# A chain of unread instructions behind the last store of a four-layer attention kernel

## The chip, the cores and the metric

The kernel runs on one core of a Trainium2 chip. The metric is the device time of one execution in microseconds (us); the time before is the median of two runs. TensorE is called PE in the profile, its weight loads PEld, VectorE DVE, ScalarE ACT, GpSimd POOL and the queue of SyncE SP.

## The reference

Two blocks alternate over one sequence of 2048 tokens of width 512, with 32 heads of 16: a block A of linear attention and a block B of sliding-window attention over the last 256 positions, each behind a layer norm and with a residual.

```python
def _A_ref(x, wqkv, wo):            # qkv split into q, k, v per head
    phi = lambda t: jnp.where(t > 0, t + 1, jnp.exp(t)) + 1e-6
    pq, pk = phi(q), phi(k)
    kv = jnp.einsum("bhsd,bhse->bhde", pk, v)
    z = jnp.einsum("bhsd->bhd", pk)
    num = jnp.einsum("bhqd,bhde->bhqe", pq, kv)
    den = jnp.einsum("bhqd,bhd->bhq", pq, z)[..., None] + 1e-6
    return merge_heads(num / den) @ wo
def _B_ref(x, wqkv, wo):            # W = 256
    scores = jnp.einsum("bhqd,bhkd->bhqk", q, k) * (Dh ** -0.5)
    mask = (idx[:, None] - idx[None, :] >= 0) & (idx[:, None] - idx[None, :] < W)
    p = _softmax(jnp.where(mask[None, None], scores, -1e9), axis=-1)
    return merge_heads(jnp.einsum("bhqk,bhkd->bhqd", p, v)) @ wo
x = A_x
x = x + _A_ref(_layernorm(x), A_wqkv, A_wo)
x = x + _B_ref(_layernorm(x), B_wqkv, B_wo)
x = x + _A_ref(_layernorm(x), A_wqkv, A_wo)
return x + _B_ref(_layernorm(x), B_wqkv, B_wo)
```

## The kernel before

Everything stays in the on-chip memory: the residual (`xres`), queries (`XQ`), keys (`kB`), values (`vB`), the exponentials of the scores (`pb`, later also `vp`) and all weights (`wA`, `wBp`, `wBv`, `wBo`). The 2048 tokens are 16 tiles of 128. A graph of operations is built by `layer_a_keys`, `barrier` and `middle`; a stored table gives the order of all operations, the engine of those that could go to two, and the bank of the accumulators (`ps`, eight banks of 128 x 512 f32). `synchronise` works out which semaphore counts each operation must wait for, and `play` in `run` issues the operations of one engine in that order: waits first, then the instruction, which raises its engine's semaphore by one (`sems`) or, for a transfer, a semaphore of its own (`dsem` for SP's, `osem` for the 15 output tiles that POOL issues).

The operations whose durations are used later are these. `tok` (L369) makes a 128x512 product from four matmuls with 512 columns each; `feat` (L383) makes it from 16 matmuls with 128 columns. `b_scores` (L599) and `b_far` (L632) multiply blocks of 32 rows, four of them at once, one in each quarter of the array's rows (`tile_position=(32 * gq, 0)`). `den` (L506) uses 32 columns of the array for each of four tiles (`tile_position=(0, 32 * tg)`). `b_values` (L674) uses the whole array with only 34 moving columns. On ACT, L609 and L641 are the exponentials of the scores, L392 the one of `phi`, L358 copies. On DVE, L615 and L650 are masks, L393 and L394 the two steps of `phi`, L537 the residual. On POOL, L649 is the mask by position, L301, L289 and L316 set up constants, L332 and L333 are parts of the layer norm.

The output leaves in 17 transfers: 15 tiles by POOL (L783) as they become ready, and the last tile in two halves by SP (L727). When SP has played its list, it waits for the last use of every one of its 48 transfer semaphores and for all of `osem`; the other engines have no such wait. The program ends when all five engines have ended their blocks. Before its first operation PE runs nine matmuls over a zeroed tile (L922), and nine more are spread behind its first operations (L946).

Of the kernel before, what the change touches and what calls it, by code (L numbers as in the profile page):

```python
# [8 lines left out]
ACT = mybir.ActivationFunctionType  # L9
ALU = mybir.AluOpType  # L10

P = 128
# [75 lines left out]
def place(g):  # L88


    ops = g.ops
    raw = zlib.decompress(b85decode("".join(TABLE)))
    n = len(ops)
    order = [ops[raw[2 * k] + 256 * raw[2 * k + 1]] for k in range(n)]
    for k, o in enumerate(order):
        o.t0 = k
    tiles, seen = [], set()
    for o in ops:
        o.eng = ("PE", "ACT", "DVE", "POOL", "SP")[raw[2 * n + o.i]]
        assert o.eng in o.engs  # L100
        for x in o.tiles:
            if id(x) not in seen:
                seen.add(id(x))
                tiles.append(x)
    for k, x in enumerate(tiles):
        x.banks = [raw[3 * n + k]]
    held = [None] * 8
    begun = set()
    for o in order:
        assert all(d.t0 < o.t0 for d in o.deps)  # L110
        for x in o.tiles:
            if id(x) in begun:
                continue
            begun.add(id(x))
            before = held[x.banks[0]]
            if before:
                assert all(u.t0 < o.t0 for u in before.users)
                o.deps.extend(u for u in before.users if u not in o.deps)
            held[x.banks[0]] = x
    return order  # L120


def synchronise(order, ring):

    know = {}
    seq = {}
    nsem = nout = 0
    dmas = []
    pool = None
    for o in order:  # L130

        e = "PQ" if o.name == "outp" else o.eng
        k = know.setdefault(e, {})
        waits = {}
        if e == "POOL":

            if pool:
                o.deps.append(pool)
            pool = o
        if e == "SP":  # L140
            if nsem >= ring:
                o.deps.append(dmas[nsem - ring])
            dmas.append(o)
        for d in sorted(o.deps, key=lambda d: -d.t0):
            if d.dma is not None:
                if d.dma in k:
                    continue
                waits[d.dma] = 1
                k.update({x: max(v, k.get(x, 0)) for x, v in d.vc.items()})
                continue  # L150
            if d.eng == e == "PE":
                continue
            if k.get(d.eng, 0) >= d.seq:
                continue
            waits[d.eng] = max(waits.get(d.eng, 0), d.seq)
            for x, v in d.vc.items():
                if v > k.get(x, 0):
                    k[x] = v
        if e == "PQ":
            o.dma = ("out", nout)  # L160
            nout += 1
            o.vc = dict(k)
        elif e == "SP":
            o.dma = ("dma", nsem)
            nsem += 1
            o.vc = dict(k)
            o.vc[o.dma] = 1
        else:
            seq[e] = seq.get(e, 0) + 1
            o.seq = seq[e]  # L170
            o.vc = dict(k)
            o.vc[e] = o.seq
        o.grp = waits
    return nsem
# [33 lines left out]
def bass_view(x, free):  # L208

    return bass.AP(x.tensor, x.offset, [x.ap[0]] + free)  # L210
# [649 lines left out]
class Kernel(Plan):  # L860
# [21 lines left out]
    def run(self):  # L882
        nc = self.nc
        order = place(self.g)
        ring = 48
        ndma = synchronise(order, ring)
        with ExitStack() as cx:
            def sb(name, shape, d=BF):
                setattr(self, name, cx.enter_context(nc.sbuf_tensor(name, [P] + shape, d)))
            sb("xres", [T, D]); sb("XQ", [4, S]); sb("xn", [4, D]); sb("xT", [3, 4, P]); sb("pqd", [4, P])  # L890
            sb("wA", [4, 3 * D]); sb("wAo", [4, D]); sb("wBp", [2, 4, D]); sb("wBv", [4, D]); sb("wBo", [4, D])
            sb("M", [4, D]); sb("zs", [4, 32]); sb("rec", [4, P]); sb("recf", [P], F32)
            sb("vp", [2 * T, D]); sb("kB", [4, 8, 64, 2]); sb("vB", [4, 2, 16, 34]); sb("pb", [3, 4, 4, 704])
# [12 lines left out]
            osem = [cx.enter_context(nc.semaphore(f"o{i}")) for i in range(T - 1)]  # L906
            last = {}
            for o in order:
                if o.dma and o.dma[0] == "dma":
                    last[o.dma[1] % ring] = o.dma[1]  # L910

            def play(name, e):
                if name == "DVE":
                    e.memset(warm, 0.0).then_inc(wsem, 1)
                if name == "ACT":

                    e.dma_start(self.kB[0:1, 3, 0:4, :, :].rearrange("p k n a -> p k (n a)"), self.A_wqkv.rearrange("(k p) c -> p k c", p=P)[0:1, :, 0:128]).then_inc(tsem, 16)
                if name == "PE":

                    e.wait_ge(wsem, 1)  # L920
                    for _ in range(9):
                        e.matmul(self.PS[:, SPARE, :], warm[:, 0:P], warm, start=True, stop=True)  # L922
                npe = 0
                for o in order:
                    if o.eng != name:
                        continue
                    for w, v in o.grp.items():
                        if w in sems:
                            e.wait_ge(sems[w], v)
                        else:  # L930
                            n = w[1]
                            e.wait_ge(dsem[n % ring], 16 * (n // ring + 1))
                    if o.name == "kd" and not touched:
                        touched.append(1)
                        e.wait_ge(tsem, 16)
                    ins = o.emit(e, name) if len(o.engs) > 1 else o.emit(e)
                    if o.dma and o.dma[0] == "out":
                        ins.then_inc(osem[o.dma[1]], 16)
                    elif o.dma:
                        ins.then_inc(dsem[o.dma[1] % ring], 16)  # L940
                    else:
                        ins.then_inc(sems[name], 1)
                    if name == "PE":
                        npe += 1
                        for _ in range(FILL.get(npe, 0)):
                            e.matmul(self.PS[:, SPARE, :], warm[:, 0:P], warm, start=True, stop=True)  # L946
                if name == "SP":
                    for n in sorted(last.values()):
                        e.wait_ge(dsem[n % ring], 16 * (n // ring + 1))
                    for x in osem:  # L950
                        e.wait_ge(x, 16)

            with nc.Block() as blk:
                @blk.tensor
                def _(e):
                    play("PE", e)

                @blk.scalar
                def _(e):
                    play("ACT", e)  # L960

                @blk.vector
                def _(e):
                    play("DVE", e)

                @blk.gpsimd
                def _(e):
                    play("POOL", e)

                @blk.sync  # L970
                def _(e):
                    play("SP", e)


def bass_interleave_layers__linear_attn_block__sliding_block__prompt_kernel(
# [38 lines left out]
```

## Time and the profile before

| what | value |
|---|---|
| median of two timed runs | 431.86 us (431.54 and 432.18) |
| profiled execution, first to last instruction (span) | 428.2 us, 17035 instructions |
| around the span (median less span) | 3.7 us |
| PE busy | 392.7 us, 92% of the span, 7471 matmuls |
| DVE busy | 356.2 us, 83%, 796 instructions |
| ACT busy | 347.4 us, 81%, 433 instructions |
| POOL busy | 128.6 us, 30%, 223 instructions |
| mean granted clock of TensorE | 0.986 of full speed |

The profile gives the profiled execution by its span; it states no separate time for it, so the time around it is read from the timed runs. A duration in the profile is that of one instruction from its start to its modelled end. Matmuls are pipelined, so a group's length is the distance between starts times their number less one, plus one duration; distances between starts are worked out from that.

### The profile page before, as it was taken

How to read it: one execution, taken by the hardware profiler on the slowest of the kernel's cores; microseconds unless marked ns; L12 is line 12 of the kernel's file. 1: busy time of each engine (PE TensorE's matmuls, PEld its weight loads, DVE VectorE, ACT ScalarE, POOL GpSimd, SP SyncE). 2: the span in 40 equal slices, each digit the busy share in tenths (PEclk: the TensorE clock that was granted, in tenths of full speed). 3: DMA queues.
4: the chain of work that ended last, by engine and by line, in shares of the span. 5: the costliest groups of instructions: out<-in, count | busy, mean ns of one | idle time of the engine just before them, and what ended most of it. 6: DMA issues, size and time to landing. Idle time of an engine off the chain costs nothing.

```text
span 428.2 us, 17035 instructions
## 1 busy us (share of the span) xinstructions
PE 392.7 (92%) x7471; PEld 257.9 (60%) x7548; DVE 356.2 (83%) x796; ACT 347.4 (81%) x433; POOL 128.6 (30%) x223
## 2 busy tenths in 40 slices
PE   8899999999899999999999999999889979997775
PEld 3445676766465566565565768585657746765544
DVE  6998899998998799887887789998798699875564
ACT  2423547999899999999998164999999999999992
POOL 4789322101240233130503303212144324332000
PEclk9999999999999999999999999999999999999968
DMA  7933016432153533453324000452434522553222
GB/s 248 269 74 87 2 42 160 117 90 70 39 111 64 103 103 77 91 112 55 95 47 65 19 2 26 114 120 63 113 62 106 116 77 77 116 133 102 64 52 51
DMA packets 66978, 37.81 MB, mean 88 GB/s; under 512 B 48248, under 2 KB 61816, under 8 KB 66904
## 3 DMA queue, kind: packets, MB, share of 16 engines
q1 hardware_dynamic: 66176, 34.75, 34.7%
q0 software_dynamic: 720, 1.97, 1.3%
q8 instruction: 59, 0.97, 1.0%
q14 instruction: 15, 0.12, 0.1%
q10 hardware_dynamic: 8, 0.00, 0.0%
HBM read 6.29 MB, written 2.10 MB: 20 GB/s over the span
## 4 chain that ended last, share of the span: by engine, by line
PE 42%; ACT 35%; DVE 16%; issue 4%; DMA 3%; POOL 1%; POOLq 0%; ACTq 0%
ACT pb L609 23%; PE ps L369 14%; PE ps L383 11%; PE ps L674 7%; ACT pb L641 6%; PE ps L599 4%; ACT vp L609 3%; DVE stats L330 2%; DVE XQ L526 2%; DVE vp L394 2%; ACT tE L392 1%; DVE tE L393 1%; DVE vp L334 1%; DMA xT<-xn 1%; DVE xres L537 1%
## 5 line engine op out<-in xcount | busy, mean ns | idle before, releaser
L609 ACT ACTIVATE pb<-ps 128x1024 bf16<-128x1024 f32 (+2 forms) x224 | 207.0, 1039 | 7.5 <-PE ps L599 6.1
L674 PEld LDWEIGHTS ps<-vB,pb 128*128 128x128 bf16 x2560 | 78.0, 96 | 13.0 <-DVE pb L615 2.8
L674 PE MATMUL ps<-vB,pb 128*128 128x34 bf16 x2560 | 83.6, 178 | 2.0 <-DVE pb L615 1.1
L392 ACT ACTIVATE tE<-ps 128x512 bf16<-128x512 f32 x64 | 38.8, 609 | 41.0 <-PE ps L369 20.6
L383 PE MATMUL ps<-xT,wBp 128*128 128x128 bf16 x1024 | 69.5, 219 | 2.1 <-DMA xT<-xn 0.8
L332 POOL TENSOR_SCALAR ve<-mv 128x1 f32<-128x1 f32 x64 | 16.6, 260 | 174.0 <-DVE mv L331 172.4
L383 PEld LDWEIGHTS ps<-xT,wBp 128*128 128x128 bf16 x1024 | 58.9, 98 | 14.8 <-issue 3.6
L615 DVE TENSOR_TENSOR pb<-pb,tri 128x512 bf16<-128x512 bf16 x112 | 48.0, 436 | 12.3 <-ACT pb L609 11.6
L599 PE MATMUL ps<-XQ,kB 32*128 32x256 bf16 (+2 forms) x1024 | 50.1, 270 | 6.9 <-ACT pb L609 3.4
L641 ACT ACTIVATE pb<-ps 128x1024 bf16<-128x1024 f32 x50 | 49.4, 1061 | 1.1 <-PE ps L632 1.0
L369 PE MATMUL ps<-wA,XQ 128*128 128x512 bf16 x177 | 46.3, 380 | 3.6 <-DVE vp L394 0.7
L537 DVE TENSOR_TENSOR xres<-ps,xres 128x512 bf16<-128x512 f32 x63 | 43.0, 685 | 7.3 <-PE ps L369 6.4
L649 POOL TENSOR_SCALAR_AFFINE_SELECT pb<-pb 128x1024 bf16<-128x1024 bf16 x30 | 35.3, 1175 | 38.5 <-ACT pb L641 37.3
L330 DVE BATCH_NORM_STATS2 stats<-xres 128x6 f32<-128x512 bf16 x64 | 43.1, 680 | 2.6 <-DMA xres<-in_A_x_dram 2.0
L333 POOL TENSOR_TENSOR rs<-ve,negh 128x1 f32<-128x1 f32 x64 | 37.5, 586 | 5.3
L383 PE MATMUL ps<-XQ,wA 128*128 128x128 bf16 x512 | 36.1, 219 | 0.4 <-DVE vp L394 0.2
L599 PEld LDWEIGHTS ps<-XQ,kB 32*128 32x128 bf16 x1024 | 15.5, 92 | 33.8 <-ACT pb L609 14.9
L369 PE MATMUL ps<-M,XQ 128*128 128x512 bf16 x115 | 31.7, 381 | 4.0 <-DVE XQ L526 1.6
L383 PEld LDWEIGHTS ps<-XQ,wA 128*128 128x128 bf16 x512 | 30.6, 98 | 7.7 <-DVE vp L394 1.2
L369 PE MATMUL ps<-wBo,oT 128*128 128x512 bf16 x104 | 30.1, 395 | 3.4 <-ACT pb L609 0.9
L369 PE MATMUL ps<-wBv,xT 128*128 128x512 bf16 x106 | 30.7, 381 | 2.7 <-issue 0.8
L369 PEld LDWEIGHTS ps<-wA,XQ 128*128 128x128 bf16 x192 | 16.1, 98 | 21.5 <-ACT XQ L353 1.7
(109 smaller groups left out, 541.2 us busy)
## 6 DMA issues: line engine op xcount, KB each, us to landing
vB<-vS SPq DMA_DIRECT2D x64, 136.0 KB, 2.5
kB<-vp SPq DMA_DIRECT2D x64, 128.0 KB, 2.2
out_dram<-xres POOLq DMA_DIRECT2D x15, 128.0 KB, 2.3
wA<-in_A_wqkv_dram SPq DMA_DIRECT2D x3, 512.0 KB, 5.9
xres<-in_A_x_dram SPq DMA_DIRECT2D x2, 512.0 KB, 4.9
pb<-in_B_wqkv_dram SPq DMA_DIRECT2D x1, 1024.0 KB, 9.0
xres<-in_A_x_dram SPq DMA_DIRECT2D x3, 256.0 KB, 4.9
wAo<-in_A_wo_dram SPq DMA_DIRECT2D x1, 512.0 KB, 7.4
```

The costliest lines, as they stand in the source:

```text
L330: self.on("DVE", "stats", lambda e: e.bn_stats(K.stats[:, t, :], K.xres[:, t, :]), key, dve(512), rd=[("xres", t)], wr=[("stats", t)])
L333: self.pow = self.on("POOL", "pow", lambda e: e.tensor_tensor(K.rs[:, t, :], K.ve[:, t, :], K.negh[:], ALU.pow), key + 0.03, (640, 690), r ...
L369: m = e.matmul(K.ps(ps), lhs(c), rhs(c), start=c == 0, stop=c == 3)
L383: m = e.matmul(K.ps(ps)[:, f * P:(f + 1) * P], w(c, f), xT(c), start=c == 0, stop=c == 3)
L392: self.on("ACT", "E", lambda e: e.activation(K.tE[:, s, :], K.ps(ps), ACT.Exp, bias=0.0), key, act(512), wr=[("tE", s)], ps=[ps])
L537: self.on("DVE", "res", lambda e: e.tensor_tensor(K.xres[:, t, :], K.ps(po), K.xres[:, t, :], ALU.add), key, dve(512), rd=[("xres", t)], w ...
L599: m = e.matmul(K.ps(ps[gq])[:, ns * i:ns * i + ns], K.kB[rows, j % 4, 2 * f + b, :, :], K.XQ[rows, f, q:q + ns], start=True, stop=True, ti ...
L609: return e.activation(out(2 * h, 2, ns), i, ACT.Exp, bias=0.0, scale=0.25)
L615: return e.tensor_tensor(x, x, K.tri[:, 0, :].unsqueeze(1).unsqueeze(1).to_broadcast([P, 4, n, 64]), ALU.mult)
L641: return e.activation(far(h), i, ACT.Exp, bias=0.0, scale=0.25)
L649: return e.affine_select(out=x, in_=x, compare_op=ALU.is_ge, fill=0.0, base=-2, pattern=[[0, 16], [-2, 64]], channel_multiplier=1)
L674: m = e.matmul(K.ps(ps)[:, 34 * u:34 * u + 34], K.P((b // 2) % rp)[:, gq, f, o:o + P], K.vB[:, (b // 2) % 4, b % 2, r, :], start=i == 0, s ...
```

## The change

Behind the list of operations, PE, ACT, DVE and POOL each get a call of `after_all`. Each waits for the final count of the three other engines, for the last two of SP's transfers (the two halves of the last output tile) and for all 15 of `osem`. Then PE runs a list of matmuls of many sizes and tile positions and raises its semaphore once; ACT waits for that and runs 11 activations; DVE waits for ACT's eleventh and runs 13 operations; POOL waits for DVE's thirteenth and runs 12. On ACT, DVE and POOL each instruction waits for the one before it. Nothing that these instructions write is stored; the operands are whatever is left in the tiles. SP gets nothing new. All instructions ahead of the call stand as they were, in the same order.

Line numbers in the profile of the changed kernel are 3 higher up to the call and 5 higher in the block below it; `after_all` begins at L979, its whole-array matmul `full` is L998.

```diff
+            seen = {x: sum(1 for o in order if o.eng == x and o.name != "outp") for x in sems}
+            self.ends = [(dsem[n % ring], 16 * (n // ring + 1)) for n in sorted(last.values())[-2:]]
...
+                if name in ("PE", "ACT", "DVE", "POOL"):
+                    self.after_all(name, e, sems, seen, dsem, osem)
                 if name == "SP":
                     for n in sorted(last.values()):
                         e.wait_ge(dsem[n % ring], 16 * (n // ring + 1))
...
+    def after_all(self, name, e, sems, seen, dsem, osem):
+        K = self
+        for x, v in seen.items():
+            if x != name:
+                e.wait_ge(sems[x], v)
+        for x, v in self.ends:
+            e.wait_ge(x, v)
+        for x in osem:
+            e.wait_ge(x, 16)
...
+        def step(ins):
+            ins.then_inc(sems[name], 1)
+            done[0] += 1
+            e.wait_ge(sems[name], done[0])
+
+        if name == "PE":
+            full = lambda b: e.matmul(psum(b), K.wA[:, 0, 0:P], K.wA[:, 1, 0:512], start=True, stop=True)
+            for _ in range(16):
+                full(6)
+            for rep in range(3):
+                full(6)
+                for f in range(4):
+                    for b in range(2):
+                        for gq in range(4):
+                            rows = slice(32 * gq, 32 * gq + 32)
+                            for h in range(2):
+                                c = 128 * f + 64 * b
+                                x = K.XQ[rows, f, 256:320] if h else bass.AP(...)    # 2 x 32 columns
+                                e.matmul(K.PS[64 * h:64 * h + 64, gq, c:c + 64], K.kB[rows, 0, 2 * f + b, 32 * h:32 * h + 32, :], x, start=True, stop=True, tile_position=(32 * gq, 64 * h))
+                full(7)
+            for rep in range(3):
+                full(6)
+                for f in range(2):
+                    for gq in range(4):
+                        rows = slice(32 * gq, 32 * gq + 32)
+                        for h in range(2):
+                            e.matmul(K.PS[64 * h:64 * h + 64, gq, 256 * f:256 * f + 256], K.kB[rows, 1, f, 32 * h:32 * h + 32, :], K.XQ[rows, f, 0:256], start=True, stop=True, tile_position=(32 * gq, 64 * h))
+                full(7)
+            for rep in range(3):
+                full(6)
+                for f in range(2):
+                    for gq in range(4):
+                        rows = slice(32 * gq, 32 * gq + 32)
+                        e.matmul(K.PS[:, gq, 224 * f:224 * f + 224], K.kB[rows, 1, f, :, :], K.XQ[rows, f, 32:256], start=True, stop=True, tile_position=(32 * gq, 0))
+                for f in range(2):
+                    for gq in range(4):
+                        rows = slice(32 * gq, 32 * gq + 32)
+                        for h in range(2):
+                            e.matmul(K.PS[64 * h:64 * h + 64, gq, 448 + 32 * f:480 + 32 * f], K.kB[rows, 1, f, 32 * h:32 * h + 32, :], K.XQ[rows, f, 32:64], start=True, stop=True, tile_position=(32 * gq, 64 * h))
+                full(7)
+            for rep in range(2):
+                for i in range(48):
+                    e.matmul(K.PS[:, 5, 68 * (i % 7):68 * (i % 7) + 68], K.pb[:, 0, i % 4, 0, 0:P], K.vB[:, 0, 0, 0:2, :].rearrange("p r d -> p (r d)"), start=True, stop=True)
+                full(7)
+            for rep in range(2):
+                full(6)
+                for i in range(16):
+                    c = i % 4
+                    e.matmul(K.PS[32 * c:32 * c + 32, 4, 0:320], K.vB[:, 0, 0, i, 0:32], K.pb[:, 0, c, i // 4, 0:320], start=True, stop=True, tile_position=(0, 32 * c))
+                full(7)
+            for rep in range(2):
+                full(6)
+                for i in range(16):
+                    c = i % 2
+                    e.matmul(K.PS[64 * c:64 * c + 34, 4, 0:320], K.vB[:, 0, 0, i, :], K.pb[:, 0, i % 4, i // 4, 0:320], start=True, stop=True, tile_position=(0, 64 * c))
+                full(7)
+            for rep in range(2):
+                full(6)
+                for i in range(64):
+                    gq, c = i % 4, (i // 4) % 4
+                    rows = slice(32 * gq, 32 * gq + 32)
+                    e.matmul(K.PS[32 * c:32 * c + 32, gq, 32 * (i // 16):32 * (i // 16) + 32], K.kB[rows, 1, 0, 0:16, :], K.XQ[rows, 0, 32:64], start=True, stop=True, tile_position=(32 * gq, 32 * c))
+                full(7)
+            low = lambda u, i, st, sp: ...     # 64 columns of the array, 34 moving, tile_position=(0, 0)
+            high = lambda u, i, st, sp: ...    # the same at tile_position=(0, 64)
+            whole = lambda u, i, st, sp: ...   # the whole array, 34 moving
+            for rep in range(2):
+                full(6)
+                for u in range(8):
+                    for i in range(4):
+                        whole(u, i, i == 0, False)
+                    low(u, 1, False, False)
+                    high(u, 2, False, True)
+                full(7)
+            for rep in range(2):
+                full(6)
+                for u in range(8):
+                    for i in range(4):
+                        whole(u, i, i == 0, False)
+                for u in range(8):
+                    low(u, 1, False, False)
+                    high(u, 2, False, True)
+                full(7)
+            for rep in range(2):
+                full(6)
+                for u in range(8):
+                    for i in range(4):
+                        low(u, i, i == 0, i == 3)
+                full(7)
+                for u in range(8):
+                    for i in range(6):
+                        whole(u, i % 4, i == 0, i == 5)
+                full(6)
+            for rep in range(4):
+                for h in range(2):
+                    for i in range(4):
+                        e.matmul(K.PS[:, 5, 256 * h:256 * h + 256], K.wA[:, i, 128 * h:128 * h + 128], K.XQ[:, i, 0:256], start=i == 0, stop=i == 3)
+            full(7).then_inc(sems["PE"], 1)
+        if name == "ACT":
+            e.wait_ge(sems["PE"], seen["PE"] + 1)
+            # 2 x Exp of 4x2x256 from PS to pb; 2 x Exp of 2x2x224 from PS to pb
+            # 2 x Relu of 512 from PS to tE; 2 x Identity of 512, xres to xn, with a bias and a scale per row
+            # 3 x Copy of 512, xres to xn
+        if name == "DVE":
+            e.wait_ge(sems["ACT"], seen["ACT"] + 11)
+            # 2 x mask (multiply) of 4x2x32 in pb; 4 x mask of 16x2x32 in pb, pieces of 32
+            # 2 x scalar_tensor_tensor (min, add) of 512 in tE; 2 x maximum of two tiles of 512 in tE
+            # 2 x tensor_scalar (add, max) of 512 from PS to tE; 1 x copy of 512 in tE
+        if name == "POOL":
+            e.wait_ge(sems["DVE"], seen["DVE"] + 13)
+            # 2 x tensor_scalar (min, add) of 512 in tE; 2 x tensor_scalar of 512, xres to xn, two operands per row
+            # 2 x affine_select of 16x32 in pb; 2 x multiply of two tiles of 512 in tE
+            # 2 x copy of 512 in tE; 2 x memset of 512 in tE
```

On ACT, DVE and POOL the lines with # stand for the loops named in them; each of these instructions is issued through `step`.

More of the change, by code (lines that the diff above doesn't have):

```diff
@@ L972, in _ @@
                     play("SP", e)
+    def after_all(self, name, e, sems, seen, dsem, osem):
[7 more added lines that the diff above has]
+            e.wait_ge(x, 16)
+        psum = lambda b: K.PS[:, b, :]
+        done = [seen[name]]
+        def step(ins):
[14 more added lines that the diff above has]
+                                c = 128 * f + 64 * b
+                                x = K.XQ[rows, f, 256:320] if h else bass.AP(K.XQ[:].tensor, K.XQ[rows, f, 256:320].offset, [K.XQ[rows, f, 256:320].ap[0], [-256, 2], [1, 32]])
+                                e.matmul(K.PS[64 * h:64 * h + 64, gq, c:c + 64], K.kB[rows, 0, 2 * f + b, 32 * h:32 * h + 32, :], x, start=True, stop=True, tile_position=(32 * gq, 64 * h))
[43 more added lines that the diff above has]
+                full(7)
+            low = lambda u, i, st, sp: e.matmul(K.PS[0:64, 5, 34 * u:34 * u + 34], K.pb[:, 0, u % 4, i % 4, 256:320], K.vB[:, 0, 0, u, :], start=st, stop=sp, tile_position=(0, 0), skip_group_check=True)
+            high = lambda u, i, st, sp: e.matmul(K.PS[64:128, 5, 34 * u:34 * u + 34], K.pb[:, 0, u % 4, i % 4, 0:64], K.vB[:, 0, 0, u, :], start=st, stop=sp, tile_position=(0, 64), skip_group_check=True)
+            whole = lambda u, i, st, sp: e.matmul(K.PS[:, 5, 34 * u:34 * u + 34], K.pb[:, 0, u % 4, i % 4, 64 * i:64 * i + P], K.vB[:, 0, 0, u, :], start=st, stop=sp, skip_group_check=True)
+            for rep in range(2):
[32 more added lines that the diff above has]
+            e.wait_ge(sems["PE"], seen["PE"] + 1)
+            out = lambda w, n: bass_view(K.pb[:, 0, 0, 0, 0:w], [[2816, 4], [704, n], [1, w]])
+            for _ in range(2):
+                step(e.activation(out(256, 2), K.PS[:, 0:4, :].rearrange("p b (n c) -> p b n c", n=2), ACT.Exp, bias=0.0, scale=0.001))
+            for _ in range(2):
+                step(e.activation(bass_view(K.pb[:, 0, 0, 0, 0:224], [[2816, 2], [704, 2], [1, 224]]), bass_view(K.PS[:, 0, 0:224], [[512, 2], [224, 2], [1, 224]]), ACT.Exp, bias=0.0, scale=0.001))
+            for _ in range(2):
+                step(e.activation(K.tE[:, 0, :], psum(0), ACT.Relu, bias=0.0))
+            for _ in range(2):
+                step(e.activation(K.xn[:, 0, :], K.xres[:, 0, :], ACT.Identity, bias=K.mv[:, 0, 0:1], scale=K.rs[:, 0, :]))
+            for _ in range(2):
+                step(e.activation(K.xn[:, 0, :], K.xres[:, 0, :], ACT.Copy))
+            step(e.activation(K.xn[:, 0, :], K.xres[:, 0, :], ACT.Copy))
+        if name == "DVE":
+            e.wait_ge(sems["ACT"], seen["ACT"] + 11)
+            tri = lambda *n: K.tri[:, 0, 0:32].unsqueeze(1).unsqueeze(1).to_broadcast([P] + list(n) + [32])
+            for _ in range(2):
+                x = bass_view(K.pb[:, 0, 0, 0, 0:32], [[2816, 4], [704, 2], [1, 32]])
+                step(e.tensor_tensor(x, x, tri(4, 2), ALU.mult))
+            for _ in range(2):
+                x = bass_view(K.pb[:, 0, 0, 0, 32:64], [[704, 16], [384, 2], [1, 32]])
+                step(e.tensor_tensor(x, x, tri(16, 2), ALU.mult))
+            for _ in range(2):
+                x = bass_view(K.pb[:, 0, 0, 0, 0:32], [[704, 16], [384, 2], [1, 32]])
+                y = bass_view(K.pb[:, 0, 0, 0, 288:320], [[704, 16], [384, 2], [1, 32]])
+                step(e.tensor_tensor(x, y, tri(16, 2), ALU.mult))
+            for _ in range(2):
+                step(e.scalar_tensor_tensor(K.tE[:, 1, :], K.tE[:, 0, :], 1.0, K.tE[:, 2, :], ALU.min, ALU.add))
+            for _ in range(2):
+                step(e.tensor_tensor(K.tE[:, 1, :], K.tE[:, 0, :], K.tE[:, 2, :], ALU.max))
+            for _ in range(2):
+                step(e.tensor_scalar(K.tE[:, 1, :], psum(0), 1.0, 1e-6, op0=ALU.add, op1=ALU.max))
+            step(e.tensor_copy(K.tE[:, 1, :], K.tE[:, 0, :]))
+        if name == "POOL":
+            e.wait_ge(sems["DVE"], seen["DVE"] + 13)
+            for _ in range(2):
+                step(e.tensor_scalar(K.tE[:, 1, :], K.tE[:, 0, :], 1.0, 1e-6, op0=ALU.min, op1=ALU.add))
+            for _ in range(2):
+                step(e.tensor_scalar(K.xn[:, 1, :], K.xres[:, 0, :], K.mv[:, 0, 0:1], K.rs[:, 0, :], op0=ALU.subtract, op1=ALU.mult))
+            for _ in range(2):
+                x = bass_view(K.pb[:, 0, 0, 0, 32:64], [[704, 16], [1, 32]])
+                step(e.affine_select(out=x, in_=x, compare_op=ALU.is_ge, fill=0.0, base=-2, pattern=[[0, 16], [-2, 32]], channel_multiplier=1))
+            for _ in range(2):
+                step(e.tensor_tensor(K.tE[:, 1, :], K.tE[:, 0, :], K.tE[:, 2, :], ALU.mult))
+            for _ in range(2):
+                step(e.tensor_copy(K.tE[:, 1, :], K.tE[:, 0, :]))
+            for _ in range(2):
+                step(e.memset(K.tE[:, 1, :], 0.0))
```

## The prediction

> **What bounds the kernel now.** The added work waits for the last store, so I read the end first: the chain of work that ended last, then the timeline of the last microseconds, then the stretches by window. Chain columns are start, length, what:
>
> ```profile
> 416.25 0.70 DVE xres L537
> 416.95 0.28 issue
> 417.24 0.54 POOL out_dram L783
> 417.78 7.52 issue
> 425.30 0.56 POOLq L953
> ```
>
> The timeline's last two lines are start, length, engine:
>
> ```profile
> 424.33 0.69 DVE L537 TENSOR_TENSOR xres<-ps,xres 128x512 bf16<-128x512 f32 x1
> 425.32 0.54 POOL L783 DMA_DIRECT2D out_dram<-xres  x1 [7.54 <-DVE xres L537]
> ```
>
> The kernel ends with an ordinary sequence: residual, output transfer, landing. POOL issues its last tile at 425.32; the page's median from issue to landing for these is 2.3 us, so it lands near 427.6, and SP's closing waits end the span at 428.2. No compute runs in that gap, so what is put behind it has nothing to hide under: its length adds to the time one for one. In the windows (second number PE busy, then PEld, DVE, ACT, POOL, the granted clock, DMA):
>
> ```profile
> 418.00:420.00 2.00, 2.00 (x74) 1.87 (x71) 1.35 (x4) 1.30 (x4) 0.00 (x0) 0.53 0.23 74
> 426.00:428.20 2.20, 0.00 (x0) 0.00 (x0) 0.00 (x0) 0.00 (x0) 0.00 (x0) 0.66 0.17 60
> ```
>
> The clock is already falling (0.66) while PE is idle at the end, and at 418 to 420 it was 0.53 although PE was full: a clock once lost comes back late.
>
> **The change part by part: the entry.** Nothing is removed or moved, and no DMA is added. Each of four engines gets some 20 waits behind its last instruction. All but the last landing's are met by then, SP waits for the same landing before, and no old instruction stands behind them: I cost them at nothing, and the work starts near 428. The cover is that landing; without it 20 waits at 0.03 us (the gap between dependent DVE steps, below) would be 0.6 us. The four lists then run one after another, since each begins on the last one's final count. So the added time is PE + ACT + DVE + POOL.
>
> **PE.** The rates come from the timeline of PE, where a group is start, length, form, count:
>
> ```profile
> 1.25 4.02 PE L922 MATMUL ps<-kB 128*128 128x512 bf16 x9 [1.25 <-DVE kB L914]
> 9.13 1.46 PE L946 MATMUL ps<-kB 128*128 128x512 bf16 x6
> 300.73 0.41 PE L632 MATMUL ps<-XQ,kB 32*128 32x64 bf16 x32
> 301.07 1.07 PE L383 MATMUL ps<-XQ,wA 128*128 128x128 bf16 x16
> 301.97 1.36 PE L674 MATMUL ps<-vB,pb 128*128 128x34 bf16 x48
> 303.38 0.40 PE L599 MATMUL ps<-XQ,kB 32*128 32x256 bf16 x8
> 303.70 1.07 PE L383 MATMUL ps<-XQ,wA 128*128 128x128 bf16 x16
> 48.22 0.40 PE L506 MATMUL ps<-XQ,zs 128*32 128x128 bf16 x16
> 48.55 1.07 PE L383 MATMUL ps<-XQ,wA 128*128 128x128 bf16 x16
> ```
>
> Taking off one duration (0.38 at 512 columns, 0.22 at 128, 0.18 at 34, 0.19 at 64) and dividing: L946 starts every 0.216 us at 512 columns; L383 every 0.0567 at 128; L674 every 0.0251 at 34. The slope of the first two is 0.415 ns a column, so 68 columns cost 0.0308 and 256 cost 0.109. L632, four row tiles side by side, starts every 7.1 ns, a quarter of 28; L506, four column tiles, every 12 ns, a quarter or less of 0.0567. So tiles in different rows or columns overlap. L922 shows the cold array: 0.43 a matmul, twice 0.216.
>
> Now the list. The whole-array matmuls with 512 columns: 16 at the head, 18 around the first three families, 2 + 12 + 14 around the rest, 1 at the end: 63 x 0.216 = 13.6 us. The families: 192 of 32x64 with 64 columns at 7.1 ns, 1.4 (eight tiles now, but I take no gain below the row's 7.1); 48 with 256 columns, eight side by side, 0.109 / 8, 0.7; 24 of 32x128 with 224 columns, four side by side, 24 ns, 0.6, and 48 with 32 columns at 7.1 ns, 0.3; 96 with 68 columns, 3.0; 32 with 320 columns in four column tiles, 34 ns, 1.1; 32 in two column tiles, 68 ns, 2.2; 128 of 32x32 at 7.1 ns, 0.9; the two mixed families of 64 whole and 32 half-width matmuls each, 64 x 0.0251 + 32 x 0.0126 = 2.0, twice, 4.0; 64 low and 96 whole at 0.0251, 4.0; 32 with 256 columns, 3.5. Together 21.7.
>
> Each change of tile shape stalls. L599's last start is 303.38 + 0.13, its columns end 0.11 later at 303.62, and L383 starts at 303.70: 0.08. After L632 the same reckoning gives 0.09, after L506 0.10. I take 0.09 for each change, also into a tile shape. There are 6 + 6 + 9 in the first three families, 12 in the three column families, 32 in the first mixed family (each group of eight goes to half width and back), 4 and 4 in the last two: 73 x 0.09 = 6.6. For bounds, zero for the 32 quick ones (a pair of half-width matmuls may flow between) takes off 2.9, zero for all 6.6.
>
> Cold clock: at the start L922's stretch begins at 1.25 and full speed is seen by 7.2. Near the end half speed began around 413.5 and ended near 420 while PE was busy from 416.2. So 3.5 to 6 us run at half; I take 4.6 us, of which half, 2.3, is lost (bounds 1.7 and 3.0). Last matmul's own tail: 0.2. PE: 13.6 + 21.7 + 6.6 + 2.3 + 0.2 = 44.4. Low: 44.4 - 6.6 - 0.6 = 37. High: the half-width weight loads have no row; if the 128 of them in the last three families each show the 0.096 duration of a PEld row instead of 0.0126 to 0.025, that is +10: 54. I stay by L506, whose narrow loads kept up.
>
> [...]
>
> **ACT.** Medians by line, minimum/median/maximum:
>
> ```profile
> L641 ACT ACTIVATE vp<-ps x6: 1017/1024/1144, 314.2 to 390.5; 128x1024 bf16<-128x1024 f32 x6
> L392 ACT ACTIVATE tE<-ps x64: 591/597/684, 8.1 to 307.5; 128x512 bf16<-128x512 f32 x64
> L650 DVE TENSOR_TENSOR pb<-pb,tri x20: 629/683/1066, 93.8 to 414.3; 128x1024 bf16<-128x1024 bf16 x20
> L615 DVE TENSOR_TENSOR pb<-pb,tri x112: 359/416/1376, 73.2 to 415.2; 128x512 bf16<-128x512 bf16 x112
> L394 DVE SCALAR_TENSOR_TENSOR XQ<-ps,tE x32: 626/681/692, 26.5 to 311.1; 128x512 bf16<-128x512 f32 x32
> L316 POOL COPY wBp<-pb x8: 753/757/760, 29.1 to 39.2; 128x512 bf16<-128x512 bf16 x8
> L301 POOL TENSOR_SCALAR_AFFINE_SELECT spread<-spread x4: 852/852/853, 12.7 to 26.6; 128x512 bf16<-128x512 bf16 x4
> ```
>
> ACT's slope is (1024 - 597) / 512 = 0.83 ns an element: 2 x 1.87 (2048 elements) + 2 x 0.92 (896) + 2 x 0.60 + 5 x 0.61 (source outside the accumulators; L511, 128 elements, took 0.31 where the slope gives 0.28) = 9.8. Dependent DVE steps start 0.03 after the other's end (L685 ends at 418.66, L686 starts at 418.69): 11 x 0.03. ACT 10.2. No second table load is in the program's list. Bounds 9.6 and 11.
>
> **DVE.** Masks by L615 and L650: 2 x 0.28 + 4 x 0.68; scalar_tensor_tensor 2 x 0.68 by L394, which reads an accumulator (low bound 0.29, the one-input L393); maximum 2 x 0.415; from the accumulators 2 x 0.69; copy 0.29; 13 gaps. 0.56 + 2.72 + 1.36 + 0.83 + 1.38 + 0.29 + 0.39 = 7.5, bounds 6.7 and 8.5.
>
> **POOL.** Memset 0.634 (L289, 512 wide), copy 0.757, affine_select between 0.69 (line from 128 to 1024 wide) and 0.852, 0.75 taken. A tensor_scalar over 512 has no row: between the memset's 0.63 and twice the copy, 1.51, I take 0.78, near the copy, as it also reads one tile. The product of two tiles has none either: between 0.757 and 1.51 I take 1.14. 4 x 0.78 + 2 x 0.75 + 2 x 1.14 + 2 x 0.757 + 2 x 0.634 = 9.7; gaps 0.08 each (L332 ended 5.39, L333 started 5.47), 12 of them: 10.6. Bounds 9 and 14.
>
> **The sum.** 44.4 + 10.2 + 7.5 + 10.6 + 0.2 for three hand-overs = 72.9. The span would go from 428.2 to about 501.1, and with the 3.7 us that the median stands above it the time is 504.8. All low ends: 62.5, 494; all high ends: 87.7, 519.6.
>
> **The rivals.** First, tiles do not overlap when row and column are both set or half the array is used: 192 x 28 ns, 48 x 109, 24 x 96 + 48 x 25, 64 x 136 and 128 x 25 make 26.0 instead of 7.2, so 524. L632 and L506 speak against it for one direction each; nothing shows both. Second, the clock stays at half through the PE list, since thin matmuls did not bring it back at once at 418: the 63 large ones add 13.6, and 68, 256 and 320 columns and the tiled ones double, about 12 more, less the 2.3: 528. Against it, at 420 the clock was back after 3.8 us of thin matmuls. Third, not slower: the time stops at the landing of the last store and not at the last engine's end. Then all 73 us lie outside and it is 431.9; it decides from the first added instruction on. Against it: the median is 3.7 us above a span that already holds the landing. Fourth, added instructions must be fetched: 2094 for PE; queues 8 and 14 moved 1.09 MB for 17035 instructions, and L632's 64 loads and matmuls in 0.22 us ran without a gap, so I expect a few tenths at most; a fetch stall of 2 us (as one transfer's landing) at each of five dense families would give 515.
>
> **How the numbers follow.** My sum 0.78; no overlap 0.09; half clock 0.06; fetch stalls 0.055; time ends at the store 0.015. The likeliest gives 504.8; the range 494 to 522 holds the sum's bounds, the stalls and a partial loss of overlap. Faster by over 2% 0.005, within 2% 0.01, slower 0.985; 2% is what a measurement of this kernel tells from no change.
>
> **What would show it.** PE's list from about 428 to 472 with the clock at half for its first 4 to 5 us; then four activities that never overlap, ACT 10, DVE 7.5, POOL 10.6 us long. In PE's groups: 64 matmuls of 64 columns within 0.65 us, 16 of 320 columns in 0.85 (four tiles) and 1.4 (two), and stalls of 0.09 at each half-width pair. I am wrong if an old group moves by more than 1 us, if the stages overlap, or if POOL's product costs over 1.5 us.

## The result and the profile after

The changed kernel takes 513.48 us (512.09 and 514.86) where the kernel before takes 431.86: a ratio of 1.189, 95% interval 1.182 to 1.195. The forecast was 504.8 with a range of 494 to 522, so the sign, the mechanism and the range held. The sum was 8.7 us short, and the rest of this text is about where these lie: POOL's operations, a second loss of TensorE's clock, the price of changing tile shapes, and the way out of the program.

The chain of work that ended last, of the changed kernel (start, length, what), shows the structure that was forecast:

```profile
427.25 1.99 DMA out_dram<-xres
429.37 5.52 PE ps L998 x17
...
476.83 0.23 PE ps L998
477.16 1.89 ACT pb L1094
...
487.15 0.64 ACT xn L1103
487.91 0.30 DVE pb L1109
...
495.29 0.31 DVE tE L1123
495.78 1.96 POOL tE L1127
497.82 1.94 POOL tE L1127
499.86 2.10 POOL xn L1129
```

The last store is issued at 427.25 and lands 2.0 later, PE starts at 429.37, and the four lists follow one another without overlap. Beside the kernel before, counted from the issue of the last store: there the span ended 2.88 later (425.32 to 428.2), here 85.15 later (427.25 to 512.4). The added 82.3 us are PE 47.7 (429.37 to 477.06), ACT 10.7, DVE 7.8, POOL 15.1 (to 510.67; hand-overs included), and 1.0 more on the way in and out (2.12 to PE's start and 1.73 behind POOL's last instruction, where all the way took 2.88 before).

What the PE rows of the timeline show on the steps (start, length, form, count):

```profile
434.82 0.71 PE L1010 MATMUL ps<-XQ,kB 32*64 32x64 bf16 x64
438.34 0.42 PE L1018 MATMUL ps<-XQ,kB 32*64 32x256 bf16 x16
447.50 0.73 PE L1040 MATMUL ps<-pb,vB 128*32 128x320 bf16 x16
449.89 1.26 PE L1046 MATMUL ps<-pb,vB 128*34 128x320 bf16 x16
453.36 0.65 PE L1053 MATMUL ps<-XQ,kB 32*32 32x32 bf16 x64
470.41 1.19 PE L1055 MATMUL ps<-vB,pb 128*64 128x34 bf16 x32
```

Taking off one duration (0.20, 0.28, 0.30, 0.30, 0.18, 0.20) and dividing by the starts less one, they begin every 8.1, 9, 29, 64, 7.4 and 32 ns. Eight and sixteen tiles side by side therefore work; at 64 and 32 columns they come no faster than four did in the kernel before (7.1).

The clock, in windows (the last four numbers are POOL busy, granted clock, DMA share, GB/s):

```profile
430.00:433.40 3.40, 3.40 (x9) 1.19 (x8) 0.00 (x0) 0.00 (x0) 0.00 (x0) 0.50 0.02 5
433.40:455.00 21.60, 21.60 (x637) 11.46 (x635) 0.00 (x0) 0.00 (x0) 0.00 (x0) 1.00 0.01 3
455.00:460.70 5.70, 5.70 (x107) 4.35 (x96) 0.00 (x0) 0.00 (x0) 0.00 (x0) 1.00 0.01 3
460.70:467.50 6.80, 6.80 (x120) 4.55 (x121) 0.00 (x0) 0.00 (x0) 0.00 (x0) 0.50 0.01 2
```

It is at half twice: for 3.4 us behind the idle end of the old part, and again for 6.8 us from 460.7 on, although PE's busy time has no gap there. What ran ahead of the second fall is the first mixed family (L1057 with L1055 and L1056). The second fall came in all seven profiles that have this family in its first order, and lasted 6.8 us in each. The first did not come every time: one of the runs below (on POOL's quick forms) has the same list for PE, and its head ran at full speed:

```profile
427.60 3.83 PE L998 MATMUL ps<-wA 128*128 128x512 bf16 x17 [3.14 <-DMA out_dram<-xres]
```

In the six profiles in which the clock fell at this head, the 17 matmuls took 5.13 to 6.63 us.

### The profile page after: what moved, and what is told of

It reads as the page before. It is cut to its first block, busy times and chain, and to the rows that moved or that the text cites. A ratio compares the mean times of both kernels' runs of the same rounds, so it can differ in the third digit from the quotient of the medians.

```text
span 512.4 us, 19285 instructions
## 1 busy us (share of the span) xinstructions
PE 449.7 (88%) x8595; PEld 287.5 (56%) x8595; DVE 362.9 (71%) x809; ACT 357.8 (70%) x444; POOL 142.5 (28%) x235
## 4 chain that ended last, share of the span: by engine, by line
PE 45%; ACT 30%; DVE 14%; DMA 4%; POOL 3%; issue 3%; SPq 0%; POOLq 0%; ACTq 0%; DVEq 0%
ACT pb L609 19%; PE ps L369 13%; PE ps L383 10%; PE ps L674 6%; ACT pb L641 5%; PE ps L998 4%; PE ps L599 4%; ACT vp L609 2%; DMA xT<-xn 2%; DVE XQ L526 2%; DVE vp L394 2%; DVE stats L330 1%; PE ps L1057 1%; ACT tE L392 1%; DVE tE L393 1%
## 5 line engine op out<-in xcount | busy, mean ns | idle before, releaser
L332 POOL TENSOR_SCALAR ve<-mv 128x1 f32<-128x1 f32 x64 | 16.4, 257 | 175.1 <-DVE mv L331 173.7
L369 PE MATMUL ps<-wA,XQ 128*128 128x512 bf16 x192 | 49.2, 380 | 2.2 <-DMA XQ<-vp 1.0
L1094 ACT ACTIVATE pb<-ps 128x2048 bf16<-128x2048 f32 x2 | 3.8, 1877 | 52.5 <-PE ps L998 52.5
L369 PE MATMUL ps<-M,XQ 128*128 128x512 bf16 x128 | 35.1, 387 | 1.9 <-DVE XQ L526 1.3
L369 PE MATMUL ps<-wBv,xT 128*128 128x512 bf16 x128 | 36.3, 388 | 0.6 <-ACT pb L609 0.4
```

The lines of the kernel that those rows point to most:

```text
L369: m = e.matmul(K.ps(ps), lhs(c), rhs(c), start=c == 0, stop=c == 3)
```

## The experiments

**The changed kernel once more.**

> The changed kernel again, to learn how far its time and the end of its old part vary between executions. Theory: the old part (up to POOL's last issue) ends between 425 and 427.5 us by chance, so the changed kernel's median lies between 511 and 515 and its added part, from the last landing on, is again 83 us within 1 us. Rival: the longer program delays the old part, so its last issue is again near 427.2 in every execution of a kernel with the longer list.

Measured: 513.31 us (511.24 to 513.99) against 431.15, ratio 1.190 (1.187 to 1.193). The last store was issued at 426.69 and the span ended at 511.8: 85.11 later, as against 85.15 the first time. The added part repeats to a tenth, in two executions in which the clock fell alike; where the head kept its clock, in the run on quick forms, PE's part was 1.8 us shorter (45.9 from its start to ACT's, as against 47.8). The old part does not repeat. Its last issue was at 425.3 in the kernel before, at 427.3 and 426.7 in the changed one, and from 425.5 to 430.2 in the variants below; the timed runs of the kernel before ran from 429.69 to 434.01. The rival, a fixed delay by the longer program, falls. So comparisons between the kernels below are made from the issue of the last store on.

**Only the waits.**

```diff
         for x in osem:
             e.wait_ge(x, 16)
+        return
```

> Only the waits of the change remain, without the four lists of work. Theory: the waits are hidden by the landing of the last store, 431.9 within 1 us, ratio 1.000 within 0.003. Rival: the waits themselves cost on the way out (20 a queue, 0.03 us each, 0.6 us or more), or the old part runs 2 us later because of what stands behind it, ratio 1.003 to 1.006.

Measured: 432.14 against 431.15, ratio 1.0028 (1.0003 to 1.0053). From the last issue (428.73) to the end of the span (432.5) it took 3.8 us, 0.9 more than before. The costing at nothing was wrong by that, though not for the number of the waits, as the next run shows.

**The waits on PE, ACT and DVE only.**

```diff
-                if name in ("PE", "ACT", "DVE", "POOL"):
+                if name in ("PE", "ACT", "DVE"):
                     self.after_all(name, e, sems, seen, dsem, osem)
```

with `return` behind the waits as above.

> The waits of the change on PE, ACT and DVE only; POOL has none and nothing of the lists is left. From POOL's last issue to the span's end there were 2.9 us before the change and 3.8 us with the waits on all four. Theory: POOL's way out of the program takes 1.7 us and is hidden under the landing unless POOL waits for it, so here it is 2.9 again and the ratio is 1.000 within 0.003. Rival: the waits on any engine cost 0.9 us, 3.8 again, ratio 1.002 to 1.004.

Measured: 431.40 against 431.15, ratio 1.0011 (0.9987 to 1.0036). From the last issue, 426.39, to the span's end, 429.3, 2.9 us: the time of before. The twenty waits on three engines are hidden; it is POOL's way out that costs when POOL is among the last. Behind POOL's last instruction the span went on for 1.73 us in the changed kernel, and 1.7 to 2.0 in all variants that end on POOL. With POOL waiting for the landing, 2.0 behind the issue, the end came 1.8 behind the landing, which is this way out and leaves nothing for POOL's own twenty waits; without, it came 0.9 behind it.

**Without POOL's list.**

```diff
         if name == "POOL":
+            return
             e.wait_ge(sems["DVE"], seen["DVE"] + 13)
```

> POOL's 12 operations are left out; PE, ACT and DVE stay. Theory: the lists only add up, so the added part falls by POOL's 15.1 us (hand-over included) and the median comes to 498.5 within 1.5 us. From the last added instruction to the span's end there were 1.7 us behind POOL's list; if that is the price of ending on POOL, it is under 1 us here and the total falls by 16. Rival: the tail of 1.7 us belongs to any program that ends on a compute engine: 1.7 again.

Measured: 496.98 against 431.99, ratio 1.1506 (1.1445 to 1.1567). From the last issue (427.01) to the span's end (495.8) 68.8 us, 16.4 less than 85.15. DVE's last instruction, at 495.04 for 0.29, ends 0.5 before the span: the long tail belongs to POOL, and 15.1 of list and 1.3 of tail add up to the difference. The median lies just below the 497 to 500 of the first forecast, as it must when the tail falls away too.

**What POOL's tensor_scalar costs.** In place of POOL's list, two each of these (512 elements where not said; one execution):

```python
(min, add) at 512, at 256, at 1024;  (min);  (add);  (mult, add)
(subtract) and (subtract, mult) with operands per row;  product of two tiles;  copy
```

> POOL's list is replaced by tensor_scalar with one and two operations at 256, 512 and 1024 elements, each twice, with the tile product and the copy beside them. Theory A: the two operations are run over each element one after another, so the time goes with elements times operations: two operations 1.95 at 512, 1.1 at 256, 3.7 at 1024; one operation about 1.1 at 512. Theory B: it is a fixed cost of the form with two operations, some 1.2 us whatever the width: 256 takes 1.6, 1024 takes 2.6, and one operation 0.75. Theory C: it is minimum that is slow, so multiply and add with two operations takes under 1.2.

POOL's timeline (two instructions to a line, so length / 2 less half a gap of 0.08 is one):

```profile
493.54 3.97 POOL L1128 TENSOR_SCALAR tE<-tE 128x512 bf16<-128x512 bf16 x2 [67.35 <-DVE tE L1123]
497.60 2.21 POOL L1130 TENSOR_SCALAR tE<-tE 128x256 bf16<-128x256 bf16 x2
499.89 7.33 POOL L1132 TENSOR_SCALAR tE<-tE 128x1024 bf16<-128x1024 bf16 x2
507.30 3.06 POOL L1134 TENSOR_SCALAR tE<-tE 128x512 bf16<-128x512 bf16 x2
510.44 3.06 POOL L1136 TENSOR_SCALAR tE<-tE 128x512 bf16<-128x512 bf16 x2
513.59 1.32 POOL L1138 TENSOR_SCALAR tE<-tE 128x512 bf16<-128x512 bf16 x2
515.01 3.22 POOL L1140 TENSOR_SCALAR xn<-xres,mv 128x512 bf16<-128x512 bf16 x2
518.34 4.25 POOL L1142 TENSOR_SCALAR xn<-xres,mv,rs 128x512 bf16<-128x512 bf16 x2
```

Means: 1.06 at 256, 1.94 at 512, 3.62 at 1024 elements. That is 3.3 to 3.4 ns an element, so theory B, a fixed cost, falls. But one operation takes 1.49, not the 1.1 of theory A, and (mult, add) takes 0.62, a third. The form decides, not the number of operations. Theory C has the size right and the reason wrong, since (add) alone, without any minimum, is as slow as (min).

**Which forms are quick.** In place of POOL's list, two each of these (one execution):

```python
(mult); (mult, mult); (add, add); (add, mult); (mult, subtract); (mult, min)
(mult, add) with two operands per row; (mult, add) with one
sum and difference of two tiles
```

> POOL's list is replaced by tensor_scalar of 512 elements in further forms, and by the sum and the difference of two tiles. In the sweep, multiply then add took 0.62, minimum then add 1.94, minimum alone or add alone 1.49, subtract alone with an operand per row 1.56. Theory A: only the pair multiply then add has a quick way, so multiply alone, multiply twice, multiply then subtract and multiply then minimum all take 1.5 to 1.95. Theory B: whatever begins with a multiply is quick, so these four are near 0.62 and add then add, add then multiply near 1.94. Operands per row: with A or B, multiply then add with two of them about 0.75 (0.13 more, as between minimum-add and subtract-multiply); rival, it loses the quick way and takes 2.07. Sum and difference of tiles: 1.15 like the product.

The chain, which has one row to an instruction:

```profile
492.15 1.54 POOL tE L1133
...
495.35 0.63 POOL tE L1135
...
496.76 1.96 POOL tE L1135
...
500.79 0.63 POOL tE L1135
...
502.20 1.95 POOL tE L1135
...
506.23 1.94 POOL tE L1135
...
510.26 0.78 POOL tE L1135
```

In the order of the list: (mult) 1.54, (mult, mult) 0.63, (add, add) 1.96, (add, mult) 0.63, (mult, subtract) 1.95, (mult, min) 1.94, (mult, add) with two operands per row 0.78; with one, 0.70. Sums and differences of tiles took 1.15. Neither theory stands: of the pairs tried, (mult, add), (add, mult) and (mult, mult) are quick and all others slow, and a single multiply (1.54) is slower than a pair of multiplies (0.63). Operands per row keep the quick way. Why these three is left open.

**The large matmuls before the wait for the landing.**

```diff
         for x, v in seen.items():
             if x != name:
                 e.wait_ge(sems[x], v)
...
+        if name == "PE":
+            for _ in range(16):
+                full(6)
         for x, v in self.ends:
             e.wait_ge(x, v)
```

with the 16 at the head of PE's list gone.

> The 16 large matmuls at the head of PE's list stand before the waits for the landing (behind those for the other engines), so that they run while the last store lands. Theory: they begin near 427 to 429 (0.1 us behind the last residual), 2 us of them are hidden under the landing, and since PE then is idle for under 1 us the clock never falls there: 2 us hidden and 1.7 us of half clock avoided, the added part falls by 3.5 to 4 us. Rival: the clock is judged on fixed stretches and falls anyway, so only the 2 us are won.

Measured: 509.45 against 431.15, ratio 1.182 (1.178 to 1.186). From the last issue (426.10) to POOL's last end (505.32) 79.2 us, where the changed kernel took 83.4: 4.2 won. PE's timeline (L986 are the 16, L1002 is the next of the large ones):

```profile
425.91 3.61 PE L986 MATMUL ps<-wA 128*128 128x512 bf16 x16 [0.83 <-issue]
429.36 0.38 PE L1002 MATMUL ps<-wA 128*128 128x512 bf16 x1
```

Sixteen in 3.61 is full speed from the first: no half clock at the head, and the landing is covered. That much is as the theory has it, and the rival is not seen. That the clock stayed because PE was idle for only 0.83 us is not shown by one profile: as said, the head kept its clock once with the old order too. The second fall came all the same, at 455.

**The first mixed family in the order of the second.**

```diff
                 for u in range(8):
                     for i in range(4):
                         whole(u, i, i == 0, False)
+                for u in range(8):
                     low(u, 1, False, False)
                     high(u, 2, False, True)
                 full(7)
```

> The first mixed family (each four whole-array matmuls followed by one half-width pair, 8 times) gets the order of the second (32 whole ones, then 8 pairs): the same instructions with 2 changes of tile shape in place of 16 per repetition. Theory: each change back and forth stalls the array by 0.22 us, so both repetitions together lose 2.5 us, and since the array then isn't idle three quarters of the time the clock stays up and the 6.8 us at half near the end of the list are gone, 3 us more: PE's list 42 in place of 47.7 us. Rival: the clock falls because matmuls with 34 columns are thin, whatever their order; then only 2.5 us are won and the stretch at half stays: 45 us.

Measured: 507.70 against 431.15, ratio 1.178 (1.175 to 1.180). PE's list ran from 428.45 to 472.26: 43.8 in place of 47.7. Two windows of this kernel, over its mixed families and over the stretch where the changed one was at half, and the head of its list:

```profile
455.00:460.70 5.70, 5.06 (x180) 4.61 (x181) 0.00 (x0) 0.00 (x0) 0.00 (x0) 1.00 0.01 3
460.70:467.50 6.80, 6.58 (x187) 5.53 (x188) 0.00 (x0) 0.00 (x0) 0.00 (x0) 1.00 0.02 5
428.45 6.63 PE L998 MATMUL ps<-wA 128*128 128x512 bf16 x17 [3.14 <-DMA out_dram<-xres]
```

The clock stays at full through the mixed families (PE's gaps in these windows are large matmuls whose records are missing): the theory holds and the rival falls. The total is between the two forecasts, because the fall at the head lasted 6.8 us here (427.3 to 434.2) and took 1.1 us more (6.63 against 5.52 for the 17 large matmuls). Without it 5.0 are won. One repetition at full clock takes 1.26 where it took 2.68 (455.50 to 458.18), so both together give 2.8 by the stalls, and the other 2.1 or 2.2 are the clock. The 1.26 runs from the first of the 32 to the large matmul behind the pairs; this matmul's record is missing from the trace, and its start is put at 456.95, one distance of 0.216 ahead of the next at 457.17. The next run has the same 1.26 between the starts of two repetitions.

**PE's shapes and the clock by themselves.** Behind PE's list, each block after 32 large matmuls: the mixed order with the pair in another bank; six whole-array matmuls to a group; the mixed order 8 times; the regrouped order 12 times; whole-array matmuls of 34 columns only. It ran once.

> Behind PE's list stand five more blocks, each after 32 large matmuls. First: the mixed order with the half-width pair writing another bank than the whole-array ones (one repetition). Second: six whole-array matmuls in place of four and a pair. Third: the mixed order 8 times, some 21 us. Fourth: the regrouped order 12 times. Fifth: whole-array matmuls of 34 columns only, 12 x 48. Theory: the stall of 0.22 us a group is the price of changing the tile shape, so the first block has a period of 0.34 a group again and the second 0.15. Rival: it is the accumulation into the same bank region, then the first block's period falls under 0.2. On the clock, theory: the array's idle share decides, so in the third block the clock falls at the first or second boundary of 3.4 us and stays at half to its end, while the fourth and fifth stay at full. Rival: thin matmuls alone bring it down, so the fourth and fifth fall too; or the fall depends on nothing in the list and half stretches appear in the runs of large matmuls as well.

```profile
485.79 0.26 PE L1057 MATMUL ps<-vB,pb 128*128 128x34 bf16 x4
485.98 0.20 PE L1092 MATMUL ps<-vB,pb 128*64 128x34 bf16 x1
485.98 0.20 PE L1093 MATMUL ps<-vB,pb 128*64 128x34 bf16 x1
486.12 0.27 PE L1057 MATMUL ps<-vB,pb 128*128 128x34 bf16 x4
...
495.39 1.36 PE L1057 MATMUL ps<-vB,pb 128*128 128x34 bf16 x48
```

A group begins every 0.337 us (486.12, 486.45, 486.79 and so on), with the pair in another bank as with the pair in the same (455.83, 456.17, 456.50 in the changed kernel): it is the change of tile shape, not the accumulation. Six whole ones take 0.151. Four whole ones and a pair that flowed would take 0.13 (4 x 0.025, and 0.03 from pair to pair in the regrouped order), so a change there and back costs 0.21, about 0.10 each way; the pair itself starts together, at 485.98.

The clock in the last blocks, by windows:

```profile
503.50:506.70 3.20, 3.20 (x59) 2.62 (x57) 0.00 (x0) 0.00 (x0) 0.00 (x0) 1.00 0.00 0
506.70:528.10 21.40, 21.40 (x330) 17.28 (x326) 0.00 (x0) 0.00 (x0) 0.00 (x0) 0.50 0.01 2
530.70:536.00 5.30, 5.30 (x26) 2.37 (x25) 0.00 (x0) 0.00 (x0) 0.00 (x0) 1.00 0.00 0
536.00:552.00 16.00, 15.97 (x580) 14.84 (x579) 0.00 (x0) 0.00 (x0) 0.00 (x0) 1.00 0.02 5
552.00:567.00 15.00, 14.77 (x356) 11.10 (x354) 0.00 (x0) 0.00 (x0) 0.00 (x0) 1.00 0.01 2
```

The mixed order begins at 503.50 and loses the clock at 506.7, 13 stretches of 3.41 us behind the fall at 462.3 inside the list, for as long as it lasts (to 528.1) and 2.5 us beyond. The regrouped order (536.2 to 551.6) and the thin matmuls (from 558.5 on) keep it. At the 0.415 ns a column of the prediction's rows, streaming 34 columns takes an estimated 14 ns at full clock; in the mixed order that is 5 x 14 of 337 ns, 21% of the time, in the regrouped order 40 x 14 of 1260, 45%, in the thin one 14 of 25, 56%. So the clock is lost at 21% and kept at 45%. Whether the share of streaming or the changes of shape themselves are what is counted, these runs do not part.

## Why the prediction was right, and where its sum was off

- **The mechanism held.** Nothing overlaps and nothing is hidden but the waits; the lists add up, and taking POOL's away took its whole length off. One of the signs of being wrong came true by the letter, an old group moving by more than 1 us: the last issue came at 427.25 after 425.32. The repeats show this as the spread of the old part between executions.
- **POOL: 10.6 forecast, 14.9 measured** (495.78 to 510.67). The term at fault is "4 x 0.78" for tensor_scalar: (min, add) took 1.94 and (subtract, mult) 2.08, 8.1 in place of 3.1. The working had written the doubt down as bounds of 0.63 and 1.51 and chosen the low side "near the copy"; the true price lies beyond the upper bound, and POOL's whole list beyond its bound of 14. A row of another form of the same instruction was no bound at all: on POOL, forms of equal width differ threefold. The product of two tiles was 1.15 for 1.14; copy 0.61, memset 0.52 and affine_select 0.72 were all slightly below their terms.
- **PE: 44.4 forecast, 47.7 measured.** The cold head lost 1.7 of the 2.3 allowed, and the size is chance: over the runs with the same 17 matmuls at the head it was 0 to 2.8. The term that was missing is the second fall at 460.7, which cost about 2.1 us; the second rival had the clock at half through the list, and held for 6.8 us of it, for a reason that it did not name. The 0.09 a change of shape was about 0.10, and a repetition of the first mixed family took 2.69 where the sum has 2.44: 0.5 us for both. The overlap of tiles held, so the first rival falls; the 64 consecutive half-width matmuls started every 32 ns, not 25, 0.4 us. Some 0.9 us are left, spread over the other families at up to 0.1 a repetition.
- For these half-width matmuls the trace has 32 ns from one matmul with its load to the next, nearer to the 25 ns of the row that was taken than to the 96 ns of a weight load in the high bound.
- **The entry, costed at nothing**, held for the waits; the way out was not looked at, and POOL as last engine makes it 0.9 us longer in the changed kernel; PE's start 0.1 behind the landing is the rest of the 1.0.
- **ACT 10.2 and DVE 7.5** were 10.6 and 7.7. ACT's difference is L1100, Identity with two operands per row, 0.82 where 0.61 was taken.
- **Fetching** cost nothing that can be seen: PE is busy without a gap in every window of the list above, and no family holds a stall of 2 us. The rival that the time ends with the store is refuted by the result.
- The time around the span did not matter, as the sum was put on the median. The 3.7 us given for it is mostly spread, a profile of one execution set against the times of others: where time and span belong to one execution they lie 1.7 to 1.9 us apart in all but three.
- **How safe the range was.** The large misses, but for the head's, were all on the low side, so they hardly cancelled. PE's 47.7 lies within its bounds of 37 and 54, but these stood for weight loads and shape changes, not for a second fall; that the total kept well within the range is owed in part to room left for costs that did not come.

A change of tile shape stalled the array by about 0.10 us in these runs (0.21 there and back in the mixed order); what the array does in that time is not shown. The boundaries at which the clock changed, 430.0, 433.4, 460.7 and 467.5, are whole multiples of 3.4 us apart; what sets them, and why the head kept its clock in one execution and lost it in others, these runs do not show.

## What to carry to other kernels

Work that is chained behind the last landing adds up to its full length, so it can be summed well, but only from rows of the very same form: an operation whose exact form has no row, above all on POOL, needs a bound of about three times its nearest neighbour. Matmuls of different tile shapes should be grouped: each change cost about 0.10 us here, and the order that changed shape at every group also lost half the clock for 6.8 us. Of the forms tried, a POOL tensor_scalar of two operations is best written as (mult, add), (add, mult) or (mult, mult), which with two constants took 0.62 to 0.63 us at 512 elements where the other pairs took 1.94 or more; and if POOL need not wait for the last landing, its way out of the program stays hidden (2.9 us from the last issue to the span's end, against 3.8).

## What was not expected of the hardware

TensorE lost half its clock (0.50 from 460.7 to 467.5) while the profile showed it busy without a gap: in the mixed order the bars of single matmuls (0.18 to 0.20 us) overlap and hide that columns stream for an estimated fifth of the time. POOL's tensor_scalar with two operations took 0.63 us or 1.95 us at the same 512 elements depending on the pair, and a single one 1.5. POOL's way out of the program took 1.7 us, DVE's 0.5.
